# A cap of two transfers on the way early in a fused attention and MLP kernel, and 32-column halves in three groups of small products

## The chip, the cores and the metric

The kernel runs on one core of one Trainium2 chip. The metric is the device time of one execution in microseconds (us). Three runs of the kernel before are at hand, and their median is the number to compare with. One more execution was profiled, and all durations below come from it.

## The reference

Two stages are chained. The first is a delta-rule attention: per batch and head a 48 x 48 state is read by the query and then updated, token by token. Its output, 3072 tokens of 384 numbers, goes through a gated MLP.

```python
B, H, S, D = 4, 8, 768, 48
k_n = k / (norm(k) + 1e-6)
for t in range(S):
    y[t] = q[t] @ state
    state = state + beta[t] * outer(k_n[t], v[t] - k_n[t] @ state)
x = y as 3072 x 384
out = (sigmoid(x @ w_gate) * (x @ w_val)) @ w_out     # 384 -> 1536 -> 384
```

## The kernel before

**Tiling.** The 768 tokens are cut into 12 groups of 64 (`N = 12`, index `g`). A group holds 32 heads and batches, 8 of each of the four kinds (e, x) of `KINDS`; e and x say on which half of the partitions a unit lies. For each group the token-by-token recurrence is turned into small matrix products: the Gram matrix of the keys (`gram`, L287 to L299), the masked product of keys and queries (`masked`, L318 to L326), the triangular inverse (`solve_halves` for groups 0 to 2, `solve` later), the product of the keys with the state (`rest`), the three steps of the new rows (`updates`), the output rows (`rows`), the state update (`advance`), and a transposition (`flip` or `turn`). All of these are float32 products, and one call of the code leaves two pairs of weight load and matmul in the trace: 32 calls of `gram` are 64 pairs.

**The MLP** of a group is done in 12 tiles of 128 columns of the hidden layer. A step of the plan is called a slot (`slot`, at the end): an even slot 2f is a gate tile (`gate_val`, L585 for group 0 and L588 later), an odd slot is the output product of two tiles before (`outp`, L613 and L619). The attention work of the next group is put into the slots of the present one, by hand: `plan[s]` runs after the slot's product, `late[s]` after the sigmoid and the gating multiplication (`gated`), `tail[s]` last. The order on all five engines is the order of the program text (`manual_schedule`), so an instruction that waits holds everything behind it on its engine.

**Loads.** All loads are issued from SP, in program order. `load_k` and `load_q` bring keys and queries of a group, two transfers each (192 KB and 256 KB), `load_rows` one half of the rows of keys and values (384 KB) and with part 1 also beta (16 KB). `load_piece(n)` brings one of 36 weight pieces of 384 KB as packed words. `pace(ins, after)` makes an instruction wait for another. 10 pieces are loaded at the start, the next ones behind the first solve (`state[0]["joint"]`, the subtraction at L437); from piece 14 on, piece n + 6 waits for `scaled(n)`.

**Weights on their way.** `scaled(n)` unpacks piece n with two ACT instructions (L194, L196), `join(n)` puts the words together on DVE (L208), and for later groups `weight_hi` and `weight_lo` split them (L217, L224). ACT does scaled(13) and scaled(14) in slot 0, scaled(15) in slot 1, 16 in slot 2, 17 in slot 3, 18 in slot 5, and so on.

**The stretch that the change touches** is the beginning, up to slot 0. Its order on SP after the first solve is: pieces 10 and 11, q of group 1 (two), pieces 12 and 13, rows part 0 of group 1, keys of group 2 (two), piece 14, pieces 15 and 16, pieces 17 and 18. On PE it is: `gram(0)`, `masked(0)`, 12 matmuls that only keep the array busy (`busy_array`, L104), `gram(1)`, busy matmuls paced by the solve, the blocks of the solve (L425 and L416), three `updates` of group 0 with busy matmuls between (L488, L480, L488), `rows(0)` (L509), `flip` (L544), and then slot 0. `gram(2)` follows in slot 3. In `gram` each product gives 64 rows from 64 columns of the stationary operand (`n = 64`), except for group 3, which does them as two halves of 32.

**After slot 3** ACT has the copies of the state (L531, in `advance(0)`), of the Gram blocks of group 2 (L310, L315), the scaling of values (L284), the pieces, and the sigmoids (L593). In slots 9 and 10 the solve of group 1 has its block products on PE (L416: first `pz`, then `pm`); `pm` needs a transposition by DVE (L429), which in DVE's order stands behind the gating multiplication of gate tile 4 (L594) and the subtraction L468.

Of the kernel before, what the change touches and what calls it, by code (L numbers as in the profile page):

```python
# [23 lines left out]
B, H, S, D = 4, 8, 768, 48  # L24
# [6 lines left out]
J = 8  # L31
CP = 2 * J
# [4 lines left out]
def tokens_at(e, x):  # L37
    return 64 * e if x else 64 - 64 * e


def below(e):

    return 64 - 64 * e
# [17 lines left out]
def deltanet_gated_mlp(ctx: ExitStack, tc: tile.TileContext, kd, qd, kv, beta, words, out):  # L61
    nc = tc.nc
# [12 lines left out]
    kqp = [const.tile([128, 6, J, C], F32, name=f"kqp{i}") for i in range(2)]  # L75
# [15 lines left out]
    def pace(ins, after):  # L91
        if after is not None:
            tc.add_manual_dep(ins.ins, after.ins.name, mybir.DependencyInfo(mybir.DependencyClass.Sync, mybir.DependencyReason.DATA), reason="pace")
# [7 lines left out]
    def busy_array(out, n, after=()):  # L101

        for i in range(n):
            ins = nc.tensor.matmul(out=out.rearrange("q a b -> q (a b)"), lhsT=flat[:, 0:128], rhs=flat, start=True, stop=True)  # L104
            if i < len(after):
                pace(ins, after[i])

    def load_k(g):
        for e in range(2):
            nc.sync.dma_start(kqp[g % 2][64 * e:64 * e + D, 0:2].rearrange("p s c t -> p (s c t)"), kd[g, e])  # L110

    def load_q(g, after=None):
        for e in range(2):
            ins = nc.sync.dma_start(kqp[g % 2][64 * e:64 * e + 64, 2 + 2 * e:4 + 2 * e].rearrange("p s c t -> p (s c t)"), qd[g, e])
            pace(ins, after)

    def load_rows(g, part):

        st = state[g]
        if "kv" not in st:  # L120
            st["kv"] = wk.tile([128, 2, CP, D], F32, name=f"kv_{g}", tag="kv", bufs=2)
        nc.sync.dma_start(st["kv"][:, part].rearrange("p c d -> p (c d)"), kv[g, :, part * CP * D:(part + 1) * CP * D])
        if part:
            st["beta"] = wk.tile([128, 32], F32, name=f"beta_{g}", tag="beta", bufs=2)
            nc.sync.dma_start(st["beta"], beta[:, g])

    def load_group(g):
        load_k(g)
        load_q(g)
        load_rows(g, 1)  # L130
        load_rows(g, 0)
# [42 lines left out]
    def load_piece(n, after=None):  # L174
        f, w = pieces[n]
        raw[n] = wt.tile([128, PW, 2], U32, name=f"raw_{n}", tag=f"w{n}")
        ins = nc.sync.dma_start(raw[n].rearrange("p c w -> p (c w)"), words[3 * f + "gvo".index(w)])
        pace(ins, after)

    def stage(lo, hi, after=None):  # L180
        for n in range(lo, hi):
            load_piece(n, after)
# [6 lines left out]
    def scaled(n):  # L189

        half, lo, hi = words_of(n)
        nc.scalar.activation(lo.bitcast(I32), half, AF.Copy, bias=-4095.5 / 8192, scale=1 / 8192)  # L194
        h = hi.bitcast(F32)
        done[n] = nc.scalar.activation(h, h, AF.Prelu, scale=2.0 ** -112, alpha=-2.0 ** 32)  # L196
        if n + BEHIND in range(EAGER, len(pieces)):
            load_piece(n + BEHIND, done[n])
# [88 lines left out]
    def gram(g):  # L287

        kq, st = kqp[g % 2], state[g]
        st["G"] = G = wk.tile([128, 32, CP], F32, name=f"G_{g}", tag="G", bufs=1)  # L290
        st["L"] = L = wk.tile([128, CP, 32], F32, name=f"L_{g}", tag="L", bufs=2)
        pg = [ps_aux.tile([128, J, C], F32, name=f"pg_{g}_{e}", tag="aux") for e in range(2)]
        for j in range(J):
            for e, x in KINDS:
                r, n = 64 * e, 32 if g == 3 else 64
                for a in range(0, 64, n):
                    t = tokens_at(e, x) + a
                    nc.tensor.matmul(out=pg[e][t:t + n, j], lhsT=kq[r:r + D, x, j, a:a + n], rhs=kq[r:r + D, x, j], start=True, stop=True)  # L298
        return blocks_of(pg, G, L, g == 0)  # L299

    def blocks_of(pg, G, L, halves):
        for e in range(2):
            js = slice(e * J, (e + 1) * J)

            for lo, hi, o in ((0, 128, 0), (32, 64, 32), (96, 128, 32)):
                block = pg[e][lo:hi, :, o:o + 32].rearrange("q p t -> q t p")
                if halves and e:
                    nc.vector.tensor_copy(out=G[lo:hi, :, js], in_=block)
                else:
                    nc.scalar.copy(G[lo:hi, :, js], block)  # L310
                yield
        for e in range(2):
            for x in range(2):
                lo, at, o = tokens_at(e, x) + 32 * e, below(e) + 32 * e, 32 - 32 * e
                nc.scalar.copy(L[at:at + 32, x * J:(x + 1) * J], pg[e][lo:lo + 32, :, o:o + 32])  # L315
                yield

    def masked(g):  # L318

        kq = kqp[g % 2]  # L320
        pool, tag = (ps_aux, "aux") if g else (ps_out, "po")
        pp = [pool.tile([128, J, C], F32, name=f"pp_{g}_{e}", tag=tag) for e in range(2)]
        for j in range(J):
            for e, x in KINDS:
                r, t = 64 * e, tokens_at(e, x)
                nc.tensor.matmul(out=pp[e][t:t + 64, j], lhsT=kq[r:r + D, x, j], rhs=kq[r:r + D, 2 + 2 * e + x, j], start=True, stop=True)  # L326

        def masks():
            for e, x in sorted(KINDS):
                t, at = tokens_at(e, x), below(e)  # L330
                nc.vector.tensor_tensor(out=kq[at:at + 64, 2 + 2 * e + x], in0=pp[e][t:t + 64],  # L331
                                        in1=pmask[t:t + 64, e].unsqueeze(1).to_broadcast([64, J, C]), op=ALU.mult)
                yield
        return masks()
# [200 lines left out]
    def flip(g, c):  # L535

        st = state[g]
        if c == 0:
            xx = wk.tile([128, 2, KC, GT], F32R if g else F32, name=f"xx_{g}", tag=f"xx{(g + 1) % 2}", bufs=1)
            st["xh"], st["xl"] = (xx[:, i] for i in range(2))  # L540
        xh, xl, ys = st["xh"], st["xl"], st["ys"][:, c].rearrange("p h e d -> p (h e d)")
        pt = ps_aux.tile([128, KC, 128], F32, name=f"pt_{g}_{c}", tag="aux")
        for k in range(KC):
            nc.tensor.transpose(pt[:, k], ys[:, k * 128:(k + 1) * 128], ident)  # L544
        ts = slice(c * 128, (c + 1) * 128)
        if g == 0:
            (nc.vector.tensor_copy if c else nc.scalar.copy)(out=xh[:, :, ts], in_=pt)  # L547
            return
        nc.scalar.copy(xh[:, :, ts], pt)
        nc.vector.tensor_tensor(out=xl[:, :, ts], in0=pt, in1=xh[:, :, ts].bitcast(F32), op=ALU.subtract)  # L550
# [103 lines left out]
    def take(gen, n=1):  # L654
        for _ in range(n):
            next(gen, None)
# [11 lines left out]
    EN = mybir.EngineType  # L668
    ctx.enter_context(tc.manual_schedule(engines={EN.DVE, EN.PE, EN.Activation, EN.Pool, EN.SP}))
    load_k(0)  # L670
    load_rows(0, 1)
    load_q(0)
    stage(0, 3)
    load_k(1)
    stage(3, 6)
    load_rows(0, 0)
    load_rows(1, 1)
    stage(6, 10)
    half = constants()
    clear(0)  # L680
    take(gram(0), 10)
    rest(0)
    masks0 = masked(0)
    gap.append(ps_gv.tile([128, J, C], F32, name="early", tag="gv"))
    busy_array(gap.pop(), 12)
# [4 lines left out]
    second_half(half)  # L690
    lower_left(0)
    take(gram(1), 10)
    take(scale_v(0), CP)
    halves0, norms1, halves1 = solve_halves(0), norms(1), solve_halves(1)
# [2 lines left out]
        scaled(n)  # L697
    take(norms1, 11)
    take(halves0, 2)
    stage(10, 12, state[0]["joint"])  # L700
    load_q(1, state[0]["joint"])
    clear(1)
    take(masks0, 2)
# [22 lines left out]
    flip(0, 0)  # L726
    flip(0, 1)
    busy_array(gap[0], 2)
    tail = collections.defaultdict(list)
    for n, at in enumerate((0, 0, 1, 2, 3, 5, 6, 8, 9, 10, 10, 11, 11, 12, 12, 13, 14, 15, 16, 16, 17, 18, 18), 13):  # L730
        plan[at].append(lambda n=n: scaled(n))
# [20 lines left out]
    def mask_later(g, s):  # L752
        def fn():
            masks = masked(g)
            take(masks, 2)
            plan[s + 1].insert(0, steps(masks, 2))
        late[s].append(fn)
        for i in range(2):
            busy[s + i] += 1.4

    def gram_later(g, s):
        def fn():
            copies = gram(g)
            for i, n in enumerate((4, 2, 4) if g < 4 else (6, 4)):
                plan[s + 1 + i].append(steps(copies, n))
        late[s].insert(0, fn)
# [118 lines left out]
```

## Time and profile before

| what | value |
|---|---|
| median of three runs | 631.37 us (631.19 to 634.57) |
| the profiled execution: its time | 631.45 us |
| the profiled execution: its span | 629.7 us |
| granted TensorE clock | 1.00 |
| bytes moved by DMA | 41.13 MB, 17,773 packets |
| weight pieces, median from issue to landing | 6.0 us |

The span is what the trace covers; the profiled execution's own time is 1.75 us longer. PE is the TensorE matmul stream and PEld its weight loads, DVE the vector engine, ACT the scalar engine, POOL GpSimd, SP the engine that issues the loads. "L416" is line 416 of the kernel before. In a timeline a row gives start, duration from the first to the last of its instructions, engine, line, operation, tiles, count, and in brackets how long the engine sat idle before it and what ended that.

### The profile page before, as it was taken

To read this page: it belongs to the slowest core of one execution; us is meant where nothing else is said; L and a number is where in the kernel's file an instruction comes from. 1 tells how busy PE (TensorE), PEld (TensorE's weight loads), DVE (VectorE), ACT (ScalarE), POOL (GpSimd) and SP (SyncE) were. 2 spreads that over 40 slices of the span, in tenths; PEclk is the share of its full clock that TensorE was granted. 3 is DMA by queue.
4 is the path that set the end of the run, shared out by engine and by line. 5 is a ranking of instruction groups with operands and counts; after the bars stand their busy time and mean duration, and the time that the engine had idled before them with its cause. 6 is when DMAs were issued, how large, how long until landed. Compare 5 with 4: busy or idle time off the path is not lost.

```text
span 629.7 us, 25087 instructions
## 1 busy us (share of the span) xinstructions
PE 610.1 (97%) x10990; PEld 566.3 (90%) x10998; DVE 478.4 (76%) x1443; ACT 345.1 (55%) x933; POOL 40.7 (6%) x102
## 2 busy tenths in 40 slices
PE   6789999999999999999999999999999999999996
PEld 3467778899999999999999999999999999999996
DVE  5887887688978978978977977977977977963221
ACT  4889775477446446456456456456456456435222
POOL 6000000000002002002001002002002002001000
PEclk9999999999999999999999999999999999999999
DMA  8495742203113113113113103112113100100101
GB/s 260 179 303 186 248 108 70 55 2 87 28 27 87 27 28 87 28 28 86 28 29 87 27 28 88 26 29 86 28 29 86 26 4 4 26 4 2 26 1 25
DMA packets 17773, 41.13 MB, mean 65 GB/s; under 512 B 4224, under 2 KB 7296, under 8 KB 17664
## 3 DMA queue, kind: packets, MB, share of 16 engines
q1 hardware_dynamic: 17664, 39.53, 22.5%
q8 instruction: 86, 1.41, 0.9%
q14 instruction: 23, 0.19, 0.1%
HBM read 34.80 MB, written 4.72 MB: 63 GB/s over the span
## 4 chain that ended last, share of the span: by engine, by line
PE 89%; DVE 7%; issue 1%; ACT 1%; DMA 1%; ACTq 0%; SPq 0%; DVEq 0%
PE gv L588 44%; PE po L619 21%; PE gv L585 5%; PE pu L488 3%; PE po L613 3%; PE yy L509 2%; PE pg L298 2%; PE pp L326 2%; PE pk L457 2%; PE pd L527 1%; PE pk L480 1%; DVE w L224 1%; PE pm L416 1%; DMA kqp<-in_kd_dram 1%; DVE hg L402 1%
## 5 line engine op out<-in xcount | busy, mean ns | idle before, releaser
L588 PE MATMUL gv<-xx,w 128*128 128x256 f32 x2376 | 311.6, 285 | 0.3 <-DVE xx L550 0.3
L588 PEld LDWEIGHTS gv<-xx,w 128*128 128x128 f32 x2376 | 299.0, 191 | 4.0 <-DVE xx L550 0.6
L619 PE MATMUL po<-w,h 128*128 128x384 f32 x792 | 162.7, 341 | 0.0
L619 PEld LDWEIGHTS po<-w,h 128*128 128x128 f32 x792 | 133.7, 188 | 1.2
L599 ACT CAST h<-sg 128x256 fp32r<-128x256 f32 x132 | 53.5, 405 | 116.0 <-DVE sg L594 115.7
L593 ACT ACTIVATE sg<-gv 128x256 f32<-128x256 f32 x144 | 54.9, 381 | 110.8 <-PE gv L588 103.4
L594 DVE TENSOR_TENSOR sg<-sg,gv 128x256 f32<-128x256 f32 x144 | 60.1, 417 | 66.2 <-ACT sg L593 65.9
L354 DVE TENSOR_TENSOR tmp<-X,gp 128x126 f32<-128x126 f32 (+22 forms) x279 | 73.4, 263 | 8.2
L357 DVE TENSOR_TENSOR X<-X,tmp 128x126 f32<-128x126 f32 (+22 forms) x279 | 72.3, 259 | 8.3
L604 DVE TENSOR_TENSOR h<-sg,h 128x256 fp32r<-128x256 f32 x132 | 54.9, 416 | 12.5 <-ACT h L599 12.4
L564 POOL COPY x<-yt 32x192 f32<-32x192 f32 x72 | 29.4, 409 | 444.6 <-DVE yt L559 441.9
L491 ACT COPY su<-pu 32x384 f32<-32x384 f32 x92 | 43.3, 470 | 10.9 <-PE pu L488 9.1
L284 ACT ACTIVATE kv<-kv,mq 128x48 f32<-128x48 f32 x192 | 47.9, 325 | 0.0
L331 DVE TENSOR_TENSOR kqp<-pp,pmask 64x512 f32<-64x512 f32 x48 | 33.0, 688 | 1.5 <-PE pp L326 0.2
L585 PE MATMUL gv<-xx,u 128*128 128x256 f32 x144 | 33.6, 384 | 0.3 <-DVE xx L547 0.3
L585 PEld LDWEIGHTS gv<-xx,u 128*128 128x128 f32 x144 | 26.7, 190 | 5.1 <-ACT xx L547 0.8
L468 DVE TENSOR_TENSOR R<-kv,pk 128x384 f32<-128x384 f32 x44 | 22.4, 550 | 10.1 <-PE pk L480 9.3
L310 ACT COPY G<-pg 32x256 f32<-32x256 f32 (+1 forms) x69 | 25.4, 368 | 8.0 <-PE pg L298 6.6
L564 ACT COPY x<-yt 32x192 f32<-32x192 f32 x72 | 25.1, 349 | 1.2
L559 DVE STREAM_TRANSPOSE yt<-ys 128x768 f32<-128x768 f32 x9 | 8.8, 979 | 19.9 <-ACT ys L515 19.9
L217 ACT CAST w<-u 128x384 fp32r<-128x384 f32 x36 | 18.0, 507 | 9.3 <-DVE w L224 9.2
L533 DVE TENSOR_TENSOR su<-su,pd 48x384 f32<-48x384 f32 x40 | 22.0, 550 | 0.5
(107 smaller groups left out, 543.6 us busy)
## 6 DMA issues: line engine op xcount, KB each, us to landing
raw<-in_words_dram SPq DMA_DIRECT2D x36, 384.0 KB, 6.0
kv<-in_kv_dram SPq DMA_DIRECT2D x24, 384.0 KB, 3.8
kqp<-in_qd_dram SPq DMA_DIRECT2D x24, 256.0 KB, 4.3
kqp<-in_kd_dram SPq DMA_DIRECT2D x24, 192.0 KB, 3.5
out_dram<-ot SPq DMA_DIRECT2D x48, 96.0 KB, 2.2
beta<-in_beta_dram SPq DMA_DIRECT2D x12, 16.0 KB, 3.5
```

The lines of the kernel that those rows point to most:

```text
L284: nc.scalar.activation(V[:, c], V[:, c], AF.Copy, scale=mq[:, c, 0:1])
L354: nc.vector.tensor_tensor(out=tmp, in0=X[:, k:16, j:j + 1].to_broadcast([128, n, j]), in1=gp[:, j:j + 1, 0:j].to_broadcast([128, n, j]), o ...
L357: nc.vector.tensor_tensor(out=X[:, k:16, 0:j], in0=X[:, k:16, 0:j], in1=tmp, op=ALU.add)
L491: (nc.vector.tensor_copy if g == 0 and x else nc.scalar.copy)(out=su[r:r + 32, 2 * x + e], in_=pu[x][r:r + 32])
L564: copy(x[32 * q:32 * q + 32, :, :, a].rearrange("q k c s -> q c k s"), yt[32 * a:32 * a + 32, :, q::4])
L585: nc.tensor.matmul(out=pg[:, o], lhsT=parts[w, f][:, k * 128:(k + 1) * 128], rhs=x[0][:, k], start=k == 0, stop=k == KC - 1)
L588: nc.tensor.matmul(out=pg[:, o], lhsT=parts[w, f][:, a, k * 128:(k + 1) * 128], rhs=x[b][:, k], start=(k == 0 and q == 0), stop=(k == KC - ...
L593: nc.scalar.activation(h, st["gv", f][:, 0], AF.Sigmoid)
L594: nc.vector.tensor_tensor(out=h, in0=h, in1=st["gv", f][:, 1], op=ALU.mult)
L599: nc.scalar.copy(hh[:, 0], st["sg", f])
L604: nc.vector.tensor_tensor(out=hh[:, 1], in0=st["sg", f], in1=hh[:, 0].bitcast(F32), op=ALU.subtract)
L619: nc.tensor.matmul(out=po[s], lhsT=hh[:, a, ts], rhs=parts["o", f][:, w], start=(f == 0 and q == 0), stop=(f == NF - 1 and q == 2))
```

## The change

Three functions are touched, and two lines switch the first part on and off.

- `in_turn(ins)` is new. While the list `behind` is not empty, a transfer is paced (the `pace` above) by the transfer two before it (`sent[-2]`). It is called for every k, q, rows and weight transfer, not for beta and not for the output. `behind.append(2)` stands right behind the first solve, `behind.clear()` just before the plan of the slots is built; so the 14 transfers named above, from piece 10 to piece 18, each get a dependency on the one two before.
- `gram`: groups 1 and 2 do their products for j < 5 and j < 3 as two halves of 32 columns; group 3 does all in halves as before, group 0 and groups from 4 on none.
- `masked`: group 0 does all its products in halves.

```diff
+    sent, behind = [], []
+
+    def in_turn(ins):
+
+        if behind and len(sent) >= behind[0]:
+            pace(ins, sent[-behind[0]])
+        sent.append(ins)
+
     def load_k(g):
         for e in range(2):
-            nc.sync.dma_start(kqp[g % 2][...], kd[g, e])
+            in_turn(nc.sync.dma_start(kqp[g % 2][...], kd[g, e]))
...
             pace(ins, after)
+            in_turn(ins)
...
-                r, n = 64 * e, 32 if g == 3 else 64
+                r, n = 64 * e, 32 if j < (0, 5, 3, J)[g if g < 4 else 0] else 64
                 for a in range(0, 64, n):
...
-                r, t = 64 * e, tokens_at(e, x)
-                nc.tensor.matmul(out=pp[e][t:t + 64, j], lhsT=kq[r:r + D, x, j], rhs=kq[r:r + D, 2 + 2 * e + x, j], start=True, stop=True)
+                r, n = 64 * e, 64 if g else 32
+                for a in range(0, 64, n):
+                    t = tokens_at(e, x) + a
+                    nc.tensor.matmul(out=pp[e][t:t + n, j], lhsT=kq[r:r + D, x, j, a:a + n], rhs=kq[r:r + D, 2 + 2 * e + x, j], start=True, stop=True)
...
     take(halves0, 2)
+    behind.append(2)
     stage(10, 12, state[0]["joint"])
     load_q(1, state[0]["joint"])
...
     busy_array(gap[0], 2)
+    behind.clear()
     tail = collections.defaultdict(list)
```

More of the change, by code (lines that the diff above doesn't have):

```diff
@@ L106, in busy_array @@
                 pace(ins, after[i])
+    sent, behind = [], []
[3 more added lines that the diff above has]
+        sent.append(ins)
     def load_k(g):
         for e in range(2):
-            nc.sync.dma_start(kqp[g % 2][64 * e:64 * e + D, 0:2].rearrange("p s c t -> p (s c t)"), kd[g, e])
+            in_turn(nc.sync.dma_start(kqp[g % 2][64 * e:64 * e + D, 0:2].rearrange("p s c t -> p (s c t)"), kd[g, e]))
     def load_q(g, after=None):
@@ L121, in load_rows @@
             st["kv"] = wk.tile([128, 2, CP, D], F32, name=f"kv_{g}", tag="kv", bufs=2)
-        nc.sync.dma_start(st["kv"][:, part].rearrange("p c d -> p (c d)"), kv[g, :, part * CP * D:(part + 1) * CP * D])
+        in_turn(nc.sync.dma_start(st["kv"][:, part].rearrange("p c d -> p (c d)"), kv[g, :, part * CP * D:(part + 1) * CP * D]))
         if part:
@@ L178, in load_piece @@
         pace(ins, after)
+        in_turn(ins)
     def stage(lo, hi, after=None):
```

## The prediction

> **What bounds the kernel now.** I read the page first, then the busy times by stretches, then the timelines of PE, ACT and DVE between 23 and 70 us, last the landings of single transfers.
>
> ```profile
> span 629.7 us, 25087 instructions
> PE 610.1 (97%) x10990; PEld 566.3 (90%) x10998; DVE 478.4 (76%) x1443; ACT 345.1 (55%) x933; POOL 40.7 (6%) x102
> ...
> q8 instruction: 86, 1.41, 0.9%
> ```
>
> ```profile
> 75.00:110.00 35.00, 35.00 (x587) 27.77 (x587) 28.43 (x80) 23.78 (x60) 0.53 (x1) 1.00 0.43 118
> 110.00:128.00 18.00, 17.18 (x590) 16.05 (x589) 11.51 (x23) 9.57 (x28) 0.00 (x0) 1.00 0.19 48
> 128.00:158.00 30.00, 29.67 (x563) 27.79 (x561) 26.54 (x81) 21.57 (x61) 0.00 (x0) 1.00 0.17 47
> 158.00:190.00 32.00, 32.00 (x693) 30.55 (x691) 25.92 (x83) 15.19 (x38) 0.00 (x0) 1.00 0.12 28
> ```
>
> (Columns: stretch, length, then busy time and count of PE, PEld, DVE, ACT, POOL, the clock, the DMA share, GB/s.) From 75 us on PE is busy 114.2 of 115.0 us, so **whatever PE loses or gains before 75 us reaches the end whole**. All that the change does lies before that: only the stretch up to 75 us has to be worked out.
>
> There PE stops in the middle of runs of small products, with the label "issue", so for no semaphore. PE's weight loads:
>
> ```profile
> 23.75 1.97 PEld L425 LDWEIGHTS pz<-mt,wide 64*64 64x64 f32 x64 [0.73 <-issue]
> 25.77 0.11 PEld L104 LDWEIGHTS <-dmask 128*128 128x128 bf16 x2
> 26.51 0.62 PEld L416 LDWEIGHTS pm<-scratch 32*32 32x32 f32 x62 [0.63 <-ACT scratch L430]
> 27.45 0.66 PEld L416 LDWEIGHTS pm<-scratch 32*32 32x32 f32 x66 [0.32 <-issue]
> 28.16 0.33 PEld L104 LDWEIGHTS <-dmask 128*128 128x128 bf16 x3
> 29.01 0.73 PEld L488 LDWEIGHTS pu<-kv,mt 32*32 32x32 f32 x59 [0.53 <-DVE mt L437]
> 31.18 0.14 PEld L488 LDWEIGHTS pu<-kv,mt 32*32 32x32 f32 x5 [1.44 <-issue]
> 31.39 0.76 PEld L104 LDWEIGHTS <-dmask 128*128 128x128 bf16 x5
> 32.58 0.85 PEld L480 LDWEIGHTS pk<-su,L 32*32 32x32 f32 x64 [0.42 <-ACT su L491]
> 33.49 0.55 PEld L104 LDWEIGHTS <-dmask 128*128 128x128 bf16 x4
> 34.71 0.13 PEld L488 LDWEIGHTS pu<-kv,mt 32*32 32x32 f32 x2 [0.67 <-DVE kv L468]
> 35.17 0.58 PEld L488 LDWEIGHTS pu<-kv,mt 32*32 32x32 f32 x48 [0.34 <-DVE kv L468]
> 36.56 0.23 PEld L488 LDWEIGHTS pu<-kv,mt 32*32 32x32 f32 x14 [0.81 <-issue]
> ```
>
> Count the pairs between the stops. From 23.75: 64 + 2 + 62 = 128. From 27.45: 66 + 3 + 59 = 128. From 31.18: 5 + 5 + 64 + 4 + 2 + 48 = 128. So the stops come every 256 instructions, and the page has (10990 + 10998) / 86 = 256 instructions for each transfer of queue q8, 1.41 MB / 86 = 16.4 KB each: **PE's code comes in blocks of 128 pairs, and PE stops where the next block is not there.** Between two stops that bind lie 27.45 - 23.75 = 3.7, 31.18 - 27.45 = 3.7 and 36.56 - 31.18 = 5.4 us; the 5.4 is the one with several loads on the way. A run of 128 small pairs needs less (62 pairs of pm take 0.74 us with their gap to the stop).
>
> **The halves.** A half adds pairs: 64 in masked(0), 5 x 4 x 2 = 40 in gram(1), 3 x 4 x 2 = 24 in gram(2), together 128, one block. So behind gram(2) the borders lie where they lay, and nothing there changes. Between gram(1) and gram(2) the borders come 104 pairs earlier, that is 24 pairs later in the next block. Price of the added pairs:
>
> ```profile
> 47.80 1.02 PEld L298 LDWEIGHTS pg<-kqp 48*64 48x64 f32 x64 [0.33 <-issue]
> 60.16 1.40 PEld L457 LDWEIGHTS pk<-su,kqp 48*32 48x32 f32 x144 [0.33 <-issue]
> ```
>
> 64 whole pairs take 1.02 us, 144 mostly halved ones 1.40: about 5 ns per added pair, 0.1 us for gram(2) on the path, 0.2 for gram(1), at most 0.6 in masked(0), where the array is slower. The last two lie beside the DVE solve, with busy matmuls behind them that wait for DVE anyway; if that cover is gone they cost 0.8. The moved borders:
>
> - In pz at pair 24, about 23.8 + 24/64 x 2.0 = 24.5. The block is one that was asked for in gram(1), 8 us before: no stop (bounds 0 to 0.5).
> - In pm at pair 62 + 24 = 86, reached near 27.5. It can be there at 24.5 + 3.7 = 28.2: a stop of 0.7 in place of the old one of 0.2. So the first solve ends 0.5 later (bounds 0.2 to 0.8).
> - In pu(0) at 59 + 24 there is no border any more: it lands 14 pairs into pk L480. Due at 28.2 + 3.7 = 31.9. pk waits for copies on DVE, so the 1.3 us stop is not all won:
>
> ```profile
> 28.27 0.69 DVE L437 TENSOR_TENSOR mt<-mt,pm 128x512 f32<-128x512 f32 x1 [0.44 <-PE pm L416]
> 28.99 1.39 DVE L331 TENSOR_TENSOR kqp<-pp,pmask 64x512 f32<-64x512 f32 x2
> 31.51 1.14 DVE L491 COPY su<-pu 32x384 f32<-32x384 f32 x2 [1.13 <-PE pu L488]
> ```
>
> L437 then ends at 29.45, L331 at 30.9, the copies at 32.1; pk starts near 32.0 instead of 32.6. 0.6 won.
> - The next border leaves pu(2) (stop 0.7) and falls into rows(0), due at 32.2 + 3.7 to 5.4 = 35.9 to 37.6, reached at 37.1: none, or 0.5. DVE then has its chain of norms and joins to do before the last copy, so of 0.7 about 0.35 is won.
>
> Slot 0 starts near 41.5 instead of 42.45: **0.95 us won** (bounds 0 and 1.5), if nothing else is late.
>
> **The cap.** It starts at the end of the first solve, J = 29.45 by the above (old 28.96). Each transfer waits for the one two before, so the 14 fall into two chains. The odd one is piece 10, q, piece 12, rows, keys, **piece 15, piece 17**; the even one ends with 14, 16, 18. Single landings, each from a window with one issue:
>
> ```profile
> raw<-in_words_dram SPq DMA_DIRECT2D x1, 384.0 KB, 3.1
> raw<-in_words_dram SPq DMA_DIRECT2D x1, 384.0 KB, 3.7
> kv<-in_kv_dram SPq DMA_DIRECT2D x1, 384.0 KB, 3.7
> kqp<-in_qd_dram SPq DMA_DIRECT2D x1, 256.0 KB, 3.6
> kqp<-in_qd_dram SPq DMA_DIRECT2D x1, 256.0 KB, 4.5
> kqp<-in_kd_dram SPq DMA_DIRECT2D x1, 192.0 KB, 2.9
> ```
>
> The 3.1 is a piece alone (window 55 to 56), the 3.7 one issued 0.9 us behind another (67.5 to 68); kv at 58.4, q at 380 and 91.5, keys at 181. In the chains a transfer runs beside one that is 1 to 2 us ahead, so I take values between: pieces 3.3 (the first 3.1), q 3.8, rows 3.4, keys 3.1. Sum of seven: 3.1 + 3.8 + 3.3 + 3.4 + 3.1 + 3.3 + 3.3 = 23.3, and 0.05 for each of six waits. **Piece 17 lands at 29.45 + 23.6 = 53.05** (bounds: all at the lower rows, with J at 29.2, 51.4; all at the upper ones, keys 3.6, 55.8). What waits for it on ACT:
>
> ```profile
> 43.98 0.55 ACT L194 ACTIVATE raw<-raw 128x384 int32<-128x384 uint16 x1 [0.84 <-DMA raw<-in_words_dram]
> ...
> 48.19 0.56 ACT L194 ACTIVATE raw<-raw 128x384 int32<-128x384 uint16 x1
> ...
> 49.74 1.93 ACT L531 COPY su<-pd 48x384 f32<-48x384 f32 x4 [0.53 <-PE pd L527]
> ...
> 62.48 0.36 ACT L593 ACTIVATE sg<-gv 128x256 f32<-128x256 f32 x1
> ```
>
> The first row is scaled(14), which already waits for its piece; the second is scaled(17), at 48.19. From there ACT has no pause but the 0.5 at L531, so the sigmoid of gate tile 4, at 62.48, comes 62.48 - 48.19 - 0.5 = 13.8 us behind piece 17. Then DVE and PE:
>
> ```profile
> 62.87 0.42 DVE L594 TENSOR_TENSOR sg<-sg,gv 128x256 f32<-128x256 f32 x1
> ...
> 66.09 0.70 DVE L429 STREAM_TRANSPOSE scratch<-mt 128x512 f32<-128x512 f32 x1
> ...
> 68.02 0.61 PEld L416 LDWEIGHTS pm<-scratch 32*32 32x32 f32 x60 [0.33 <-ACT raw L196]
> 69.06 0.68 PEld L416 LDWEIGHTS pm<-scratch 32*32 32x32 f32 x68 [0.42 <-issue]
> ```
>
> DVE's order from that sigmoid's product to the transposition that pm needs takes 66.79 - 62.87 = 3.9 us, after some 0.4 from the sigmoid's start. So pm starts no earlier than piece 17 + 13.8 + 0.4 + 3.9 = + 18.1, at 71.1; before, it started at 68.0. Behind waiting pm stands all of PE. Meanwhile its block has come, so its stop of 0.4 goes. The 0.95 won at slot 0 is waited away. **Sum: 71.1 - 68.0 - 0.4 = 2.7 us lost.** The nearer stations agree or have room: keys of group 2 land near 46.3, gram(2) is due near 46.9; gate tile 4 waits some 1.1 us for the product of tile 2, part of the same delay. I take 2.5 for small pauses that ACT's list has and that would be filled. The profiled execution, 631.45, becomes 633.95; it stands 0.1 above the median, so 633.9 us against 631.37.
>
> A rule speaks about the blocks: the Trainium skill, "Runtime: NRT & Kernel Launch", "Instruction fetch mechanics", says that code comes in 16 KiB blocks of 256 instructions and that the refill is mostly hidden. The size agrees with the 16.4 KB above, the hiding does not, with stops of 0.3 to 1.4 us; by it the halves would win nothing, and the sum, from which their win drops out, would stand but for J.
>
> **The rivals.**
> 1. *Transfers drag* (slower). With pieces at 3.7, q 4.5, rows 3.7, keys 3.6 piece 17 lands at 55.8 and the loss is 5.2: 636.6. The place is scaled(17), the price 1 us per us; it is over 0.5% (3.16 us, what a measurement here tells from no change) once the seven average 3.4 us; the forecast's average is 3.33. For: pairs issued 0.9 us apart did take 3.7 and 4.5. Against: in the chains they drift 1 us and more apart.
> 2. *The cap is free* (not slower). Once the seven average 2.9 us, piece 17 lands by 50.0 and the 0.95 stays, less 0.1 for gram(2) and 0.1 beside it: 630.7. For: only 3 of 23.6 us have to be found. Against: no weight piece quoted lands under 3.1. The Trainium skill, "DMA: Bandwidth & Descriptors", "Anatomy of one DMA", gives 2.0 us plus bytes over 436 GB/s for the GpSimd path: an estimate of 2.9 us for a 384 KB piece, which would be this case; the 3.1 row speaks against it.
> 3. *The change doesn't do what it says*: both instructions are SP's, and the dependency might be met by their order instead of the landing. Then loads run as before, the borders still move, and rows(0) may stop 0.5: 630.7 to 631.2.
>
> **Numbers.** Forecast, loss 1.0 to 3.1: 0.50. Rival 1, over 3.1: 0.28. Rivals 2 and 3: 0.11 and 0.08. Left, 0.03, a win over 0.5%: it would need all stops before 75 us gone. Likeliest's own range 632.4 to 634.5; with the rivals 630.6 to 636.4. Faster by over 0.5% 0.03, within 0.69, slower 0.28.
>
> **What would show it.** Right: no stop in the runs L488 before slot 0, one of about 0.7 in pm L416 near 27.5, slot 0 near 41.5; 14 transfers at 3 to 4.5 us each; ACT waiting for pieces 14, 15, 17 with "DMA raw", scaled(17) near 53; a wait of PE before pm near 69. Wrong: scaled(17) before 50, or PE held elsewhere (gram(2) by its keys); stops that moved to other runs; and PE's stretch behind 75 us longer than before.

## The result and the profile after

| kernel | median | runs | ratio to before, 95% interval |
|---|---|---|---|
| before | 631.08 us | 629.48 to 634.57 | |
| changed | 634.94 us | 633.70 to 636.42 | 1.0057 (1.0032 to 1.0082) |

By the ratio the change costs about 3.6 us. Two single executions in what follows, one of 836.44 and one of 1168.38 us (the profiled one of the kernel with five GpSimd passes), were disturbed as a whole; they are left out of the medians and not read.

The profiled execution of the changed kernel took 634.96 us, 3.5 more than that of before. Its lines are numbered 12 higher than before's from L331 on (L416 is L428, L585 is L597), and 10 higher just ahead of that. First the page, then the busy times by stretches (columns as in the prediction):

```profile
span 633.2 us, 25341 instructions
PE 613.1 (97%) x11118; PEld 567.4 (90%) x11126; DVE 478.6 (76%) x1443; ACT 344.7 (54%) x933; POOL 40.7 (6%) x102
...
q8 instruction: 87, 1.43, 0.9%
```

```profile
75.00:110.00 35.00, 35.00 (x577) 27.28 (x576) 29.14 (x84) 21.81 (x52) 0.53 (x1) 0.99 0.44 130
110.00:128.00 18.00, 17.42 (x519) 15.84 (x520) 10.71 (x22) 9.45 (x30) 0.00 (x0) 1.00 0.18 47
```

The added halves are the 128 pairs more (10990 to 11118) and one block of code more (86 to 87). Behind 75 us PE is as full as before, so nearly all that is lost is lost ahead of it. The PE timeline of the changed kernel shows where, with three rows of the kernel before behind it:

```profile
40.90 5.45 PE L597 MATMUL gv<-xx,u 128*128 128x256 f32 x24 [0.47 <-ACT xx L559]
46.28 1.47 PE L308 MATMUL pg<-kqp 48*32 48x64 f32 x88
...
57.55 2.86 PE L597 MATMUL gv<-xx,u 128*128 128x256 f32 x12 [0.45 <-DVE sg L606]
...
70.53 1.28 PE L428 MATMUL pm<-scratch 32*32 32x32 f32 x128 [2.26 <-DVE scratch L441]
71.73 2.43 PE L625 MATMUL po<-u,sg 128*128 128x384 f32 x4
73.96 3.62 PE L597 MATMUL gv<-xx,u 128*128 128x256 f32 x12
...
78.79 0.88 PE L500 MATMUL pu<-R,mt 32*32 32x48 f32 x64
```

```profile
69.78 1.56 PE L613 MATMUL po<-u,sg 128*128 128x384 f32 x4
71.17 2.75 PE L585 MATMUL gv<-xx,u 128*128 128x256 f32 x12
...
75.14 0.88 PE L488 MATMUL pu<-R,mt 32*32 32x48 f32 x64
```

Slot 0 starts at 40.90 instead of 42.45, 1.55 us earlier. Then small waits eat that, and pm, the masked product of stage 1, starts at 70.53 instead of 68.03 after PE has waited 2.26 us for it. The two groups of products behind it, the same as before in shape and count, take 2.43 instead of 1.56 and 3.62 instead of 2.75 us: 1.74 us more. At pu the loss is 78.79 - 75.14 = 3.65, and the end is later by nearly the same, 3.5 (span 633.2 against 629.7). So it goes in every profile: in the 13 that are read, the time of the execution is 555.3 to 556.5 us more than the start of this pu. What is lost ahead of pu reaches the end.

Why the products are slower stands in the stretches of 1 us behind the wait; the last three figures of a row are the granted clock, the DMA share and GB/s:

```profile
70.50:71.50 1.00, 0.97 (x116) 1.00 (x118) 0.96 (x4) 1.00 (x4) 0.00 (x0) 1.00 0.66 178
71.50:72.50 1.00, 1.00 (x38) 0.70 (x25) 0.93 (x5) 1.00 (x4) 0.00 (x0) 0.89 0.93 328
72.50:73.50 1.00, 1.00 (x3) 0.51 (x2) 1.00 (x3) 1.00 (x3) 0.00 (x0) 0.50 1.11 361
...
74.50:75.50 1.00, 1.00 (x4) 0.81 (x3) 0.96 (x4) 0.00 (x0) 0.00 (x0) 0.50 0.97 356
75.50:76.50 1.00, 1.00 (x5) 0.83 (x5) 0.93 (x5) 0.00 (x0) 0.00 (x0) 0.90 0.87 277
```

The clock is cut to half from about 72.3 to 75.7, some 3.4 us, and is whole again after that. Half the speed for 3.4 us is 1.7 us lost, the 1.74 of the two groups.

What pm waits for goes back to the loads. ACT of the changed kernel:

```profile
46.88 0.56 ACT L204 ACTIVATE raw<-raw 128x384 int32<-128x384 uint16 x1 [5.13 <-DMA raw<-in_words_dram]
...
48.86 0.56 ACT L204 ACTIVATE raw<-raw 128x384 int32<-128x384 uint16 x1 [0.69 <-DMA raw<-in_words_dram]
...
51.18 0.56 ACT L204 ACTIVATE raw<-raw 128x384 int32<-128x384 uint16 x1 [1.32 <-DMA raw<-in_words_dram]
...
52.40 0.55 ACT L204 ACTIVATE raw<-raw 128x384 int32<-128x384 uint16 x1
...
66.06 0.36 ACT L605 ACTIVATE sg<-gv 128x256 f32<-128x256 f32 x1
```

These are scaled(14) to scaled(17) and the sigmoid of gate tile 4. ACT waits 5.13 us for piece 14, and piece 17 lands at 52.37. The row at 52.40 has no wait: in this execution ACT comes from piece 16, for which it waited 1.32 us, just as piece 17 lands, so the two chains tie. In the other profiles with a cap of two throughout ACT does wait for piece 17, 0.50 to 1.18 us. The seven transfers of the odd chain, each from a window that holds its issue alone, in their order:

```profile
raw<-in_words_dram SPq DMA_DIRECT2D x1, 384.0 KB, 2.9
...
kqp<-in_qd_dram SPq DMA_DIRECT2D x1, 256.0 KB, 4.0
...
raw<-in_words_dram SPq DMA_DIRECT2D x1, 384.0 KB, 3.7
...
kv<-in_kv_dram SPq DMA_DIRECT2D x1, 384.0 KB, 3.2
...
kqp<-in_kd_dram SPq DMA_DIRECT2D x1, 192.0 KB, 2.6
...
raw<-in_words_dram SPq DMA_DIRECT2D x1, 384.0 KB, 3.4
...
raw<-in_words_dram SPq DMA_DIRECT2D x1, 384.0 KB, 3.5
```

Their sum is 23.3 us, spent two at a time. A single transfer lands sooner than before (a median of 5.9 us for the 13 pieces that the window from 30 to 52 us holds there, 3.6 for the 8 here), but fewer bytes come: 4.47 MB in that stretch against 6.81.

### The profile page after: what moved, and what is told of

Its sections match the earlier page's. It is cut to its first block, busy times and chain, and to the rows that moved or that the text cites. A ratio compares the mean times of both kernels' runs of the same rounds, so it can differ in the third digit from the quotient of the medians.

```text
span 633.2 us, 25341 instructions
## 1 busy us (share of the span) xinstructions
PE 613.1 (97%) x11118; PEld 567.4 (90%) x11126; DVE 478.6 (76%) x1443; ACT 344.7 (54%) x933; POOL 40.7 (6%) x102
## 4 chain that ended last, share of the span: by engine, by line
PE 84%; DVE 6%; DMA 5%; ACT 3%; issue 1%; SPq 1%; ACTq 0%; DVEq 0%
PE gv L600 44%; PE po L631 21%; DMA raw<-in_words_dram 3%; PE gv L597 3%; PE pu L500 3%; PE yy L521 2%; PE po L625 2%; PE pp L338 2%; PE pg L308 2%; PE pk L469 2%; PE pk L492 1%; PE pd L539 1%; DVE w L234 1%; PE pm L428 1%; DMA kqp<-in_qd_dram 1%
## 5 line engine op out<-in xcount | busy, mean ns | idle before, releaser
L597 PE MATMUL gv<-xx,u 128*128 128x256 f32 x144 | 34.7, 393 | 1.3 <-DVE sg L606 0.7
L597 PEld LDWEIGHTS gv<-xx,u 128*128 128x128 f32 x144 | 27.3, 195 | 7.4 <-DVE sg L606 2.1
L204 ACT ACTIVATE raw<-raw 128x384 int32<-128x384 uint16 x36 | 20.1, 558 | 7.9 <-DMA raw<-in_words_dram 7.9
```

The costliest lines, as they stand in the source:

```text
L597: nc.tensor.matmul(out=pg[:, o], lhsT=parts[w, f][:, k * 128:(k + 1) * 128], rhs=x[0][:, k], start=k == 0, stop=k == KC - 1)
```

## The experiments

Diffs are against the changed kernel unless they say otherwise. Every kernel was timed beside the kernel before, with a median of 631.17 us there (631.33 beside the kernels with GpSimd passes and the cap raised to three), and ratios are to that.

**The halves alone, and the cap alone.**

```diff
-    behind.append(2)
+    pass
```

> The halves stay, the cap is taken out. Theory (the cap makes weight pieces 16 and 17 late, ACT and DVE pass that on, PE waits 2.3 us before pm and then runs at a granted clock of 0.76): no wait of PE before pm, clock 1.0 behind it, slot 0 near 41 us, 630.2 us (ratio to before 0.997 to 1.000). Rival (the loss comes from the 128 added pairs or the moved borders of the code blocks): the loss stays, 634 to 635 us.

```diff
-                r, n = 64 * e, 32 if j < (0, 5, 3, J)[g if g < 4 else 0] else 64
+                r, n = 64 * e, 32 if g == 3 else 64
...
-                r, n = 64 * e, 64 if g else 32
+                r, n = 64 * e, 64
```

> The cap stays, all halves are taken out. Theory: the chain of landings starts at the same end of the first solve, so piece 17 lands near 52 and nearly all of the loss stays: 634.3 to 635.5 us. The stops of PE come back at the old places, the second (36.6 us before) shorter than 0.67, since fewer loads are on the way. Rival (the halves cost the time): 631 us.

The halves alone: 631.37 us, ratio 1.0003 (0.9987 to 1.0020), no gain, where 630.2 was expected. The cap alone: 637.08 us, 1.0075 (1.0050 to 1.0099). So the cap carries the whole loss. With it alone the median is higher than that of the changed kernel, though the intervals overlap, and above the 634.3 to 635.5 expected: piece 17 landed at 55.01 and not near 52. PE's products with the halves alone:

```profile
46.67 1.47 PE L308 MATMUL pg<-kqp 48*32 48x64 f32 x88
...
51.40 0.92 PE L597 MATMUL gv<-xx,u 128*128 128x256 f32 x3 [0.40 <-issue]
52.15 1.45 PE L625 MATMUL po<-u,sg 128*128 128x384 f32 x4
```

Slot 0 started at 41.32, 1.13 earlier than before, in spite of a stop of 0.88 in the weight loads of rows(0). Then gram(2) took 1.47 instead of 1.16, and PE stopped in the middle of a gate tile, where before it did not; the next product came at 52.15, before at 52.30. A win at slot 0 is there, and 10 us later it is gone. Of the cap alone, ACT's scaled(17) and the wait it leads to:

```profile
55.03 0.56 ACT L204 ACTIVATE raw<-raw 128x384 int32<-128x384 uint16 x1 [1.18 <-DMA raw<-in_words_dram]
```

```profile
73.15 1.28 PE L428 MATMUL pm<-scratch 32*32 32x32 f32 x128 [2.09 <-DVE scratch L441]
```

Piece 17 at 55.01 plus the prediction's 18.1 is 73.1: pm starts there.

**A cap of three.**

```diff
-    behind.append(2)
+    behind.append(3)
```

> Halves, and a cap of three. Theory: in three chains piece 17 is the fifth of its chain, 28.8 + 3 + 4 x 4.2 = 48.6 us, before 50.1, so no wait before pm: 630.4 us. Rival (three share the same bytes per us, and piece 17 lands as late as with two): 634 us or more.

631.15 us, 0.9991 (0.9972 to 1.0011): the loss is gone, and nothing is won, where 630.4 was expected. Piece 17 landed at 48.77, pm did not wait, slot 0 started at 40.85. PE:

```profile
61.96 0.82 PE L428 MATMUL pz<-mt,scratch 32*32 32x32 f32 x72
64.16 0.68 PE L428 MATMUL pz<-mt,scratch 32*32 32x32 f32 x56 [1.38 <-issue]
```

The first part of pz comes 1.14 us earlier than before (63.10), its second, behind a border of a code block, only 0.47 (64.63 there). What was won is waited away in a code stop that is 1.38 us long instead of 0.71.

**Dummy products in the wait.** In the solve of stage 1, ahead of `blocks(pm, D, Z)`; measured twice, the second time beside the changed kernel itself:

```diff
+        if g == 1:
+            busy_array(pm, 6)
         blocks(pm, D, Z)
```

> As the changed kernel, with six matmuls of 128 x 512 that only keep the array busy put right before pm in the solve of group 1, where PE waits 2.3 us. Theory (the pause of 2.3 us lowers the granted clock to 0.76 for some 7 us, 1.7 us of the loss): clock 1.0 behind pm, 633.2 us. Rival (the products behind pm are slow because loads run at 306 GB/s there): no gain, 634.9 us.

> The changed kernel once more, as the base of this call. Both theories: 634.9 us (633.7 to 636.4), piece 17 landing near 52.4, the masked product of stage 1 starting 18.1 us later (near 70.5) after a wait of the TensorE of about 2.2 us, and the granted clock near 0.76 for the seven microseconds behind it.

> The changed kernel with six dummy matrix products ahead of the masked product of stage 1, so that the TensorE does not stand still there (its wait stays, the pause of its array goes). Theory (the slower clock behind the wait costs 1.7 us: 2.43 instead of 1.56 in the pair of the fourth Gram product, 3.62 instead of 2.75 in the values): where piece 17 lands as in the kernel of the same call, the time is 1.7 us below it, near 633.2, with a clock of 1.00 between 70 and 77. Rival (the slower clock is given back later or lies beside a code stop): the same time as it, within 0.5.

The changed kernel again: 635.42 us, 1.0059 (1.0036 to 1.0082), piece 17 at 53.37, pm at 71.57 after a pause of 2.13, clock 0.76 over the seven microseconds behind it. With the dummies: 635.02 the first time, 1.0057 (1.0035 to 1.0079), and 634.94 the second, 1.0059 (1.0038 to 1.0079). PE with the dummies the second time, two rows of the changed kernel again behind it, and with the dummies the seven microseconds from pm on:

```profile
69.13 1.24 PE L104 MATMUL pm<-dmask 128*128 128x512 bf16 x5
71.61 1.28 PE L428 MATMUL pm<-scratch 32*32 32x32 f32 x128 [1.24 <-DVE scratch L441]
72.82 1.56 PE L627 MATMUL po<-u,sg 128*128 128x384 f32 x4
74.21 2.75 PE L599 MATMUL gv<-xx,u 128*128 128x256 f32 x12
...
78.18 0.88 PE L502 MATMUL pu<-R,mt 32*32 32x48 f32 x64
```

```profile
71.57 1.28 PE L428 MATMUL pm<-scratch 32*32 32x32 f32 x128 [2.13 <-DVE scratch L441]
...
79.84 0.88 PE L500 MATMUL pu<-R,mt 32*32 32x48 f32 x64
```

```profile
71.60:78.60 7.00, 6.99 (x186) 5.32 (x190) 6.73 (x23) 5.26 (x13) 0.00 (x0) 1.00 0.94 307
```

The wait is the same and the pause shorter; the clock stays whole and the two groups take their old 1.56 and 2.75 us. So it is the pause that halves the clock. These two executions also meet the condition of the expectation, that piece 17 lands alike (53.45 and 53.37). pm starts at 71.61 and 71.57, pu 1.66 us earlier with the dummies, and the times are 634.26 and 635.80 us: the 1.5 to 1.7 us reach the end.

The medians do not show this (0.5 us between them), and there the expectation failed. One reason is on record: not every execution of the changed kernel loses the clock. Of its twelve, seven have a mean clock of 0.995 or 0.996 and average 635.6 us, five have 0.998 or 0.999 and average 634.3. Over all runs the mean clock was 0.998 with the dummies and 0.9965 to 0.997 without, which is 0.8 us of 633; what takes that back is not shown. In the profile of the first time with dummies the loads started later (a stop of 0.67 us in pm of stage 0, piece 17 at 54.69), before the dummies run; whether that is chance stays open.

**The cap lifted earlier, or raised.** The first of these:

```diff
     load_k(2)
+    behind.clear()
```

> The changed kernel with the cap lifted behind the transfer of the keys, so that pieces 14 to 18 are issued at once and only ten transfers are held to two at a time. Theory (the loss is the landing of piece 17 plus 18.1 us against a TensorE that is ready at 68.2): piece 17 lands near 49, below 50.1, so no wait stands before the masked product of stage 1, no clock is lost, and the time is 631.0. Rival (the cap costs by holding the earlier ten back): 633 or more, with a wait of over 1 us there.

634.64 us, 1.0059 (1.0037 to 1.0080): as slow as the changed kernel, and the theory as written failed. The cap held nine transfers, not ten; then six pieces went out within 2.4 us (43.84 to 46.20), and piece 17 landed at 52.5, not at 49. PE did not wait for it:

```profile
49.16 2.21 PE L597 MATMUL gv<-xx,u 128*128 128x256 f32 x9
53.45 0.92 PE L597 MATMUL gv<-xx,u 128*128 128x256 f32 x3 [2.08 <-issue]
54.20 2.51 PE L625 MATMUL po<-u,sg 128*128 128x384 f32 x4
56.50 3.43 PE L597 MATMUL gv<-xx,u 128*128 128x256 f32 x12
```

```profile
53.40:60.40 7.00, 6.95 (x21) 5.04 (x22) 5.84 (x22) 6.84 (x21) 0.00 (x0) 0.76 0.59 194
```

It stopped for 2.08 us at the border of a code block, the one that cost the halves alone 0.40 and the changed kernel nothing; the block's own transfer began at 51.22, behind the burst. And that stop, with no wait for data in it, halved the clock too.

```diff
     load_k(2)
+    behind[0] = 3
```

> The changed kernel with the cap raised from two to three behind the transfer of the keys, so that pieces 14 to 18 go neither one beside another nor all at once. Theory (the loss is either piece 17 after 50.1 or a burst that a code block stands behind, and here is neither): piece 17 lands near 50.5, the masked product waits for under 0.7 us, the clock stays at 1.00, no code stop of over 1 us in the gate tiles, and the time is 631.6. Rival (the cap of two over the first ten transfers costs by itself): 633.5 or more.

633.91 us, 1.0030 (1.0008 to 1.0053), between the two. Piece 17 landed at 52.48 and not at 50.5, since pieces 16 to 18 took 5.1 to 5.4 us each:

```profile
70.80 1.93 PE L428 MATMUL pm<-scratch 32*32 32x32 f32 x128 [2.57 <-DVE scratch L441]
```

Here the twelve runs fall apart by their clock: seven of 631.86 to 633.94 us with 0.998 or 0.999 and five of 634.90 to 636.76 with 0.992 to 0.996 (the profiled one among them). The means lie 2.8 us apart, the clocks 0.0040, which is 2.5 us of 633.

```diff
-    behind.append(2)
+    behind.append(3)
...
-    behind.clear()
```

> The halves with a cap of three that is never lifted, so that all later loads are held to three at a time as well. Theory (the stop between the two halves of the next masked product, 1.38 us with a cap of three that is lifted and 0.71 before, is a code block that waits behind the loads of the next stages): with fewer loads on the way the stop falls to 0.7 or less and the 0.6 us won reach the end: near 630.5. Rival (the block is due by its own chain from the block before): the stop stays above 1.2 and the time is 631.1 or, where a later load comes late, more.

631.12 us, 0.9999 (0.9984 to 1.0013). In the profile the stop in pz fell to 0.65 us, and that execution took 629.38:

```profile
63.31 0.68 PE L428 MATMUL pz<-mt,scratch 32*32 32x32 f32 x56 [0.65 <-issue]
```

But it is the fastest of its twelve (629.38 to 633.42), and the median is that of before. No version was found that beats the kernel before.

**The pause by itself.** The kernel before, with passes of GpSimd ahead of pm that change no value; five, five with the dummies of above behind them, and three:

```diff
+        if g == 1:
+            for _ in range(5):
+                nc.gpsimd.affine_select(out=D, in_=D, pattern=[[0, CP], [0, 32]], compare_op=ALU.is_ge, fill=0.0, base=1, channel_multiplier=0)
         blocks(pm, D, Z)
```

> The kernel before, with no cap and no halves, and with five passes of GpSimd over the second operand of the masked product of stage 1 that keep every value (5 x 0.72 us, with handoffs some 3.7 us behind the transposition that ends at 66.8). The product starts near 70.5 instead of 68.0, the TensorE stands still for about 2.5 us. Theory (a pause of over 2 us lowers the granted clock to about 0.8 for seven microseconds, and that reaches the end): 631.2 + 2.5 + 1.7 less the stop of 0.3 in this product = 635.1, clock 0.75 to 0.83 between 70 and 77. Rival (the clock fell in the changed kernel through something else, such as the load on the DMA, or is given back): 633.4, clock 1.00.

> The same with six dummy matrix products ahead of the masked product, so that the wait is as long and the pause of the TensorE's array 1.2 us shorter. Theory: clock 1.00, the price of the wait alone, 633.4, 1.7 us below the kernel without the dummies. Rival: as that kernel, within 0.5.

> As the first kernel of this call with three passes of GpSimd instead of five: the masked product starts near 69.0, after a pause of about 1.0 us. Theory (a pause near 1 us leaves the clock alone): clock 1.00, time 631.2 + 1.0 less 0.3 = 631.9. Rival (any pause here lowers the clock): 633 or more, with a clock below 0.95 between 70 and 77.

Five passes: 636.6 us, 1.0071 (1.0045 to 1.0097). Five with dummies: 636.71 us, 1.0072 (1.0049 to 1.0094). Three: 633.03 us, 1.0027 (1.0006 to 1.0048). These are 1.1 to 3.3 us above what was expected (635.1, 633.4, 631.9). The passes were longer than I had taken them, in the profile with three:

```profile
66.58 2.75 POOL L434 TENSOR_SCALAR_AFFINE_SELECT scratch<-scratch 128x512 f32<-128x512 f32 x3 [42.26 <-DVE scratch L429]
```

0.92 us each instead of 0.72. So the dummies no longer covered the wait (2.01 us of pause were left, and the clock was 0.76 over seven microseconds), and that pair tells nothing apart. The three passes made about the pause that five were meant to make:

```profile
69.37 1.84 PE L416 MATMUL pm<-scratch 32*32 32x32 f32 x128 [2.20 <-POOL scratch L434]
71.14 2.45 PE L616 MATMUL po<-u,sg 128*128 128x384 f32 x4
```

```profile
69.30:76.30 7.00, 6.93 (x145) 5.54 (x146) 4.63 (x16) 2.30 (x7) 0.49 (x2) 0.76 0.90 275
```

No cap and no late load is in this kernel, and after 2.20 us of pause the clock falls as in the changed one: the cause is the pause, not the transfers. A pause of 1.0 us behind GpSimd was not made; the 1.24 with the dummies and the 1.38 of the code stop above left the clock at 1.00, so the rival that any pause lowers it isn't borne out.

## Why the prediction came out as it did

The forecast of 633.9 us lies 1 us under the measured 634.94. That is inside the range with the rivals (630.6 to 636.4) and above the likeliest case's own (632.4 to 634.5). The loss of 3.6 us is larger than the 1.0 to 3.1 of that case, and the ratio of 1.0057 belongs to "slower", which had 0.28, though its interval reaches into "within 0.5%", which had 0.69.

The path was the right one: late pieces, ACT, DVE, pm, all of PE. The cap was not free, and each of the 14 transfers went out with one other under way. Rival 1 did not come in this profile (the seven average 23.3 / 7 = 3.33 us, as forecast), but it was close. In the second profile of the same kernel they average 3.46, over the 3.4 at which that rival begins, and 3.68 with the cap alone. The size of the loss is rival 1's; here it came from the clock.

- **The blocks.** Borders came where the count of pairs put them: in pm of stage 0 behind pair 86 in the profiles where PE stopped there, and pu(0) ran through. What failed in this part is "it can be there at 24.5 + 3.7 = 28.2: a stop of 0.7": the 3.7 is no constant. In the changed kernel there was none, and in the others it was 0 to 0.67. Thus "L437 then ends at 29.45" was 28.76, outside the step's bounds (0.2 to 0.8 later than before's 28.96):

```profile
26.51 1.41 PEld L428 LDWEIGHTS pm<-scratch 32*32 32x32 f32 x128 [0.63 <-ACT scratch L442]
...
28.81 0.75 PEld L500 LDWEIGHTS pu<-kv,mt 32*32 32x32 f32 x64 [0.53 <-DVE mt L449]
```

- **The win at slot 0** was 1.55 us, where 0.95 was forecast (bounds 0 and 1.5), and it was waited away as said.
- **"About 5 ns per added pair, 0.1 us for gram(2)"** was too low: 24 pairs cost 0.31 us, 13 ns each. It was no term of the end, since PE waited behind it.
- **"Piece 17 lands at 29.45 + 23.6 = 53.05".** It landed at 28.76 + 23.61 = 52.37. The chain was right to 0.01 us, all of the 0.7 is the start of the chain. That closeness is luck: single terms were off both ways (piece 12 took 3.7 and not 3.3, the keys 2.6 and not 3.1), and in the four other profiles with a cap of two throughout the same chain took 24.4 to 26.1 us. The upper bound of 55.8 comes out only with J at 29.2 and without the sum's own pauses of 0.3; with both as in the sum it is 56.4.
- **"Piece 17 + 18.1".** 52.37 + 18.1 = 70.47, and pm started at 70.53. In four other profiles with a wait there the rule holds to 0.1 us (73.15 for 73.11, 71.57 for 71.47, 72.87 for 72.79, 71.61 for 71.55), and to 0.2 in the one with the cap raised to three (70.80 for 70.58).
- **"Its stop of 0.4 goes"**: it did, pm ran its 128 pairs in one run, and from its start to that of the next group it took 0.55 us less.
- **The sum** of 2.5 us has no term for the clock; this is the step that failed. 70.53 - 68.03 - 0.55 = 1.95 is what the wait cost, 1.74 what the halved clock cost, together 3.7 of the 3.65 at pu. An early start of the chain (0.7 us gained) and the missing term (1.7 lost) cancelled in part: the number is nearer than its working deserves, and that too is luck.

That the lost clock was the missing term is shown in the trace, by the pause that was shortened (clock whole) and by the pause that was made without any cap (clock halved). That it reaches the end is shown by the two profiled executions with pm at 71.6, 1.54 us apart. For the medians it is not shown: with the dummies they stayed within 0.5 us.

A rule of the Trainium skill speaks of this: "TensorE: Matmul & The Clock Gate", "HAM oscillation — how this bites in real kernels", warns of idle gaps of the array over 3.4 us, after which it runs at half clock. The half clock agrees with the trace (0.50); the bound does not, as pauses of 2.01 to 2.57 us were enough in seven profiled executions here.

## What to carry to other kernels

A wait on an engine that has no slack can cost more than its length once TensorE stands still for about 2 us: count the half clock behind it as well (here 1.7 us), and look at the granted clock in windows of 1 us, since the mean over the kernel (0.996) hides it. A cap on the transfers trades the latency of each against the bytes per us: work out when the last needed one lands, and follow it through every engine to the bound, as piece 17 + 18.1 us did here. And a win ahead of a border of a code block is only a win if the next block comes earlier too.

## What the runs showed of the hardware

- **The clock halves for 3.4 us behind a pause of about 2 us**, whatever made it: a wait for DVE (2.09, 2.13, 2.26, 2.57 us), one for GpSimd (2.01, 2.20) or a code stop (2.08); near 17 us too, behind waits of 1.85 (five passes with dummies) and 2.20 (the cap alone). Pauses of 0.84, 1.24, 1.38, 1.58 and 1.77 us left it at 1.00.
- **The clock changes only in steps of 3.413 us, and a pause counts by what of it lies in one step.** By the trace's own record of the clock, there is always a whole number of them between two changes (in the changed kernel 17 at full clock, then 1 at half, then 163). In the 13 profiles, a step in which PE's timeline stands still for 1.66 us or more was always followed by the half clock. Steps with 1.55 or less were not, but for one with 1.32 among small products (five passes with dummies); at 1.65 both happened. Of the 2.26 us before pm 1.66 lay in one step, the least that always sufficed, and of the 1.77 us no step held more than 1.30. What exactly is counted isn't settled by these runs.
- **A clock of 1.00 in a view can mean no record.** This record begins 12 to 16 us into the span. Before that the views show 1.00, but the dummies of 128 x 512 follow each other every 0.43 us, and every 0.22 us after.
- **Code blocks stand behind loads.** The same border in a gate tile cost nothing in the changed kernel (two loads under way), 0.40 us with the halves alone (no cap) and 2.08 behind a burst of six pieces. The block's own transfer began 2.0, 2.4 and 4.2 us behind the start of gram(2). That the loads ahead of it hold it up is read from this order; the moment at which a block is asked for is not in the trace.
- **A deep queue delays each transfer more than it speeds their sum.** With the halves alone, the pieces issued between 30 and 45 us took a median of 7.8 us, kv 8.5 and keys 8.8, against 3.7, 3.2 and 2.9 in the changed kernel, while 304 GB/s were moved against 195.
